# Four attention layers on one core: weight blocks asked for two ahead, layer-norm rows normed one ahead, one more unread matmul per row tile in layers 3 and 4

## The chip, the core and the metric

The kernel runs on one core of a Trainium2 chip. A core has a matrix engine (TensorE, PE in the profile; the loading of its stationary operand is listed apart as PEld), a vector engine (VectorE, DVE), a scalar engine (ScalarE, ACT), a general engine (GpSimd, POOL) and an engine that here only starts transfers (SyncE, SP). Each runs its own stream of instructions in order, and semaphores make one wait for another. The metric is the device time of one execution in microseconds (us), and lower is better. Before the change it is 2338.05 us, the median of four runs from 2328.9 to 2343.6 us.

## What is computed

A sequence of 2048 positions with 640 features goes through four layers. Each is `x = x + attention(layernorm(x))` with 32 heads of 20 features. Layers 1 and 3 use the weights A and a sliding window of 256 keys, layers 2 and 4 the weights B and all 2048 keys without a mask.

```python
def layer(x, wqkv, wo, windowed):                 # x: (1, 2048, 640)
    q, k, v = split_heads(layernorm(x) @ wqkv)    # 32 heads of 20
    s = einsum("bhqd,bhkd->bhqk", q, k) * 20 ** -0.5
    if windowed: s = where(0 <= qi - ki < 256, s, -1e9)
    return x + merge_heads(softmax(s) @ v) @ wo

x = layer(layer(A_x, A_wqkv, A_wo, True), B_wqkv, B_wo, False)
x = layer(layer(x,   A_wqkv, A_wo, True), B_wqkv, B_wo, False)
```

`layernorm` subtracts the mean of a position's 640 features and divides by `sqrt(var + 1e-5)`.

## The kernel before

**Tiling.** The code counts layers `l` from 0 to 3, so layer 3 of the text is `l = 2`. Positions are cut into four chunks `c` of 512, a chunk into four row tiles of 128 positions, and heads into eight groups `g` of four. A unit is one (layer, chunk, group). Its scores come in banks: one head's 512 queries against 128 keys fill one PSUM bank (128 partitions x 512 values). There are eight banks; score tiles use banks 0 to 2 and 3 to 5 by turns (banks 3 to 6 in a wide tile), and bank 7 collects probabilities times values. In the early part, in which every second tile has two banks, all other matmuls share banks 5 and 6; after `end_early` (line 265), which comes when the layer norms of layers 1 and 2 are done, they have bank 6 alone.

**The main loop** (from line 1210) is worked through when the kernel is built; what the chip gets is one fixed stream for each engine. One pass is called a tick here. It issues the score matmuls of the next tile of up to three banks (line 1244), one Exp on ACT for that tile (line 1275), then some other work, then the probability-times-value matmuls of an earlier tile (line 1308), then the mask products on DVE for windowed tiles (line 1344). There are 1635 ticks, and units of neighbouring layers are interleaved, so that the layer norms, projections and output projections of one layer stand between the attention ticks of another.

**The other work** consists of generators, called tasks. `pump` (line 241) lets the task that is due first advance while a credit lasts; the credit grows at each tick by a rate that is worked out from the work left and when it is due. A task gives the credit back what it costs (`yield ("pe", 0.22)`), or steps aside for n ticks (`yield ("wait", n)`). `take_m` (line 253) hands out a PSUM bank for such work; after `end_early` a bank that was given back in a tick is to be had in the next tick only, so that at most one such piece of work is done per tick.

**Tasks that the change touches:**

- `t_ln` (line 376) is one chunk's layer norm. POOL works out the reciprocal deviation (lines 387 and 390) from statistics that DVE left. Then for each of the four row tiles DVE norms the row into the tile `xn` (line 399; the pool `xnp` has two buffers), the task waits a tick, PE transposes the 128x640 row in five 128x128 pieces into a bank (line 410), and DVE, or ACT in the early part, copies the bank to `xnT` (`evac`, lines 302 and 304). In layers 1 and 2 two unread matmuls come ahead of the transposes.
- `unread` (line 609) multiplies a 128x128 identity with a 128x512 tile into a bank that nobody reads, and adds 1.0 to `heat`. `keep_clock` (line 623) does the same at the end of a tick while the `heat` that the tick's work and a carry of at most 3.0 add up to is under a minimum. These unread matmuls are there for the TensorE clock, which the page lists as the granted clock.
- `take_w` (line 329) hands a 128-column block of the q and k weights to a projection (`t_block`, line 500, and `t_qk_first`, line 485). `worder[l, n]` lists the blocks of layer l in order of use, with n = 0 for q and 1 for k. A block is fetched by `get_w` (line 312), in layer 1's first chunk by copies on DVE and a memset on POOL, otherwise by a transfer that POOL starts. `wtiles` holds the blocks that are fetched and not yet taken. When a block is taken and none of its list is in `wtiles`, the next of the list is fetched. The pool `wqkp` has eight buffers.
- A projection's result is copied to `st` and stored by a transfer that POOL starts as well (line 509), as are the value tiles (line 467). POOL's stream holds these stores, the weight fetches and the layer norms' two small operations, in one order.

In the code below `x_sb` holds the residual stream, `ps` the eight banks, and `ka` serves at times as the output of wide Exp tiles.

Of the kernel before, what the change touches and what calls it, by code (L numbers as in the profile page):

```python
# [49 lines left out]
def kernel(  # L50
# [202 lines left out]
    def take_m():  # L253
        while True:
            b = min(mfree, key=mfree.get)
            if mfree[b][0] <= state["tick"]:
                mfree[b] = (1 << 30, 0)
                return b
            yield ("wait", 1)

    def drop_m(b):
        mseq[0] += 1
        mfree[b] = (state["tick"] + (not state["early"]), mseq[0])
# [22 lines left out]
    def room(*tags):  # L286
        while any(live[t] + tags.count(t) > cap[t] for t in tags):
            yield ("wait", 1)
        for t in tags:
            live[t] += 1  # L290
        state["running"].holds = True
# [8 lines left out]
    def evac(out_, in_):  # L300
        if state["act"]:
            nc.scalar.copy(out=out_, in_=in_)
        else:
            nc.vector.tensor_copy(out=out_, in_=in_)  # L304


    wtiles = {}
# [4 lines left out]
    def get_w(l, n, c, i):  # L312

        t = wqkp.tile([P, KD, P], BF16, name="wqk", tag="wqk")
        wtick[l, n, c, i] = state["tick"] + 4
        if l or c:
            a = n * D + i * P
            nc.gpsimd.dma_start(out=t[:], in_=wq_view[l % 2][:, :, a : a + P])
            return t
        tv = t[:].rearrange("p c (j m) -> p c j m", j=4)  # L320
        nc.gpsimd.memset(tv[:, :, :, DH:32], 0.0)
        src = raw[:, :, n * D + 80 * i : n * D + 80 * (i + 1)]
        nc.vector.tensor_copy(
            out=tv[:, :, :, 0:DH], in_=src.rearrange("p c (j e) -> p c j e", j=4)
        )
        wtick[l, n, c, i] = 0
        return t

    def take_w(l, n, c, i):
        key, order = (l, n, c, i), worder[l, n]  # L330
        if key not in wtiles:
            wtiles[key] = get_w(*key)
        while state["tick"] < wtick[key]:
            yield ("wait", 1)
        at = order.index(key)
        order.pop(at)
        wt = wtiles.pop(key)
        if at < len(order) and not any(e in wtiles for e in order):
            wtiles[order[at]] = get_w(*order[at])
        return wt  # L340

    staging = []
# [33 lines left out]
    def t_ln(l, c):  # L376
        while ("x", l, c) not in ready:
            yield ("wait", 1)
        yield from room("xnT", "ln")
        for n in (1, 0):  # L380
            order = worder[l, n]
            if order and not any(e in wtiles for e in order):
                wtiles[order[0]] = get_w(*order[0])
        users[l, c] = 9 if (l, c) == (0, 0) else (11, 12, 11, 11)[l]
        mv = mvs.pop((l, c))
        rstd = lnp.tile([P, 4], F32, name="rstd", tag="rstd")
        nc.gpsimd.tensor_scalar(  # L387
            out=rstd[:], in0=mv[:, :, 1], scalar1=EPS, scalar2=1.0, op0=ALU.add, op1=ALU.mult
        )
        nc.gpsimd.tensor_tensor(out=rstd[:], in0=rstd[:], in1=nhalf[:], op=ALU.pow)  # L390
        yield ("wait", 2)
        nmr = lnp.tile([P, 4], F32, name="nmr", tag="nmr")
        nc.vector.scalar_tensor_tensor(
            out=nmr[:], in0=mv[:, :, 0], scalar=-1.0, in1=rstd[:], op0=ALU.mult, op1=ALU.mult
        )
        xt = xtp.tile([P, KD, C], BF16, name="xnT", tag="xnT")
        for i in range(4):
            xn = xnp.tile([P, D], BF16, name="xn", tag="xn")
            nc.vector.tensor_scalar(
                out=xn[:], in0=x_sb[:, 4 * c + i, :],  # L400
                scalar1=rstd[:, i : i + 1], scalar2=nmr[:, i : i + 1],
                op0=ALU.mult, op1=ALU.add,
            )
            yield ("wait", 1)
            mb = yield from take_m()
            for _ in range(2*(l<2)):
                unread(mb)
            trp = ps[:, mb, :].bitcast(BF16)[:, 0 : KD * P].rearrange("p (c m) -> p c m", c=KD)
            for dc in range(KD):
                nc.tensor.transpose(  # L410
                    out=trp[:, dc, :], in_=xn[:, dc * P : (dc + 1) * P], identity=ident[:]
                )
            evac(xt[:, :, i * P : (i + 1) * P], trp)
            drop_m(mb)
            yield ("pe", 0.4)
        xnT[l, c] = xt
        live["ln"] -= 1
        ready.add(("xnT", l, c))
# [66 lines left out]
    def t_qk_first(l, c, g):  # L485
        while ("xnT", l, c) not in ready:
            yield ("wait", 1)
        yield from room("qa", "ka", "w", "w")
        wt = yield from take_w(l, 0, c, g)
        q = qa_free.popleft()  # L490
        yield from project(wt, xnT[l, c], lambda: q[:])
        wt = yield from take_w(l, 1, c, g)
        k = ka_free.popleft()
        yield from project(wt, xnT[l, c], lambda: k[:])
        live["w"] -= 2
        qa[c, g], ka[c, g] = q, k
        used(l, c)
        ready.add(("qk", l, c, g))

    def t_block(l, n, c, b):  # L500

        while ("xnT", l, c) not in ready:
            yield ("wait", 1)
        yield from room("w")
        wt = yield from take_w(l, n, c, b)
        yield from project(wt, xnT[l, c], staged)
        rows = slice(b * P, (b + 1) * P)
        dst = k_d[l][rows, c * C : (c + 1) * C] if n else q_d[l][c, rows, :]
        nc.gpsimd.dma_start(out=dst, in_=staging.pop())
        live["w"] -= 1  # L510
        used(l, c)
        ready.add(("qk"[n], l, c, b))
# [65 lines left out]
    def push_layer(l, c):  # L578

        need = [first_use(l, c, g) for g in range(G)]  # L580
        if c or l:
            push(("ln", l, c), t_ln(l, c), need[0], 1.6)
        if l % 2:
            halves = ((0,), (1,)) if l == 1 else ((0, 1),)
            for h in halves:
                push(("v", l, c, *h), t_v(l, c, h), need[4 * h[0]], 2.8 * len(h))
        elif c or l:
            push(("v", l, c), t_v(l, c, (0, 1)), need[0], 5.6)
        if c or l:
            for b in range(KD):  # L590
                g = b * P // 80
                for n in (1, 0):
                    worder[l, n].append((l, n, c, b))
                    first = index[l, c, g, PARTS[l][0] if l % 2 and c == 0 else None]
                    first = need[g] if n else first
                    push(("qk"[n], l, c, b), t_block(l, n, c, b), first, 1.1)
            return
        for g in range(G):
            for n in (0, 1):
                worder[l, n].append((l, n, c, g))  # L600
            push(("qk", l, c, g), t_qk_first(l, c, g), need[g], 2.2)
            if g == 0:
                push(("v", l, c), t_v(l, c, (0, 1)), need[0], 5.6)
# [5 lines left out]
    def unread(b):  # L609

        nc.tensor.matmul(  # L611
            ps[:, b, :], lhsT=ident[:], rhs=masks[:, 0, :], start=True, stop=True
        )
        state["heat"] += 1.0
# [522 lines left out]
    with tc.manual_schedule():  # L1137
# [17 lines left out]
        while n < last_layer:  # L1155
            size = 2 if len(tiles) % 2 and narrow(banks[n][0]) else 3
            u = banks[n][0]
            at = placed.setdefault(id(u), [])
# [51 lines left out]
        while ended is None or t < ended + 8:  # L1210
# [3 lines left out]
            if t < len(tiles) or banks:  # L1214
# [54 lines left out]
                i = 0  # L1269
                while i < n_b:  # L1270
# [8 lines left out]
                    i = k  # L1279
# [52 lines left out]
            if t > 0 and masked is not None:  # L1332
                cur_, pt_ = masked
                i = 0
                while i < len(cur_):
# [12 lines left out]
                    i = k  # L1348
# [36 lines left out]
```

## Time and profile before

The times are those of the page: the profiled execution took 2340.73 us by the device's clock, and the span of its trace, from its first to its last instruction, is 2339.0 us; 1.7 us lie around it.

| What | Value |
|---|---|
| median of the four runs | 2338.05 us |
| profiled execution, its span | 2340.73 us, 2339.0 us |
| ACT busy | 2178.4 us, 93% of the span |
| PE busy | 2016.7 us, 86% |
| DVE busy | 1463.5 us, 63% |
| POOL busy | 271.1 us, 12% |
| Exp on ACT (line 1275) | 2099.8 us in 1641 instructions |
| unread matmuls (line 611) | 256.5 us in 768 instructions |
| row norms on DVE (line 399) | 29.8 us, 60 of 497 ns |
| transposes of the layer norm (line 410) | 30.1 us in 150 listed records, 300 with their loads |
| weight fetches started by POOL (line 318) | 150, landing 3.7 us (B) and 3.3 us (A) after issue |

The page's row of busy tenths cuts the span into 40 slices of 58.5 us. PE's durations in it are from start to modelled end, and matmuls overlap, so a PE share near 90% does not say that the array does nothing but useful work. In the row of the granted clock, 9 stands for a share of 90% or more, and the last third of the span, where layer 4 is alone, has 5. Windows of the trace give by stage:

| Stretch of the span | PE busy | DVE busy | ACT busy | granted clock |
|---|---|---|---|---|
| 0 to 130 us | 112.57 | 87.37 | 92.60 | 0.95 |
| 130 to 400 us | 251.68 | 191.29 | 238.61 | 0.99 |
| 400 to 560 us | 140.94 | 67.06 | 150.71 | 1.00 |
| 560 to 1690 us | 974.28 | 652.39 | 1074.42 | 0.96 |
| 1690 to 2339 us | 537.19 | 465.38 | 622.07 | 0.55 |

The fifteen layer norms that `t_ln` does lie between 51 and 1569 us. The seven of layers 1 and 2 are done by 442 us, the eight of layers 3 and 4 start at about 568, 794, 842, 1077, 1125, 1342, 1408 and 1563 us.

### The profile page before, as it was taken

Reading aid. Unit: us, or ns where it says so; the run is one execution under the profiler, and the core shown is the slowest. Engines: PE = TensorE matmul, PEld = TensorE weight load, DVE = VectorE, ACT = ScalarE, POOL = GpSimd, SP = SyncE. Lnnn points to the kernel's source line nnn. Section 1 sums busy time; section 2 is a strip of 40 time slices with the busy share of each in tenths; the row PEclk is TensorE's granted clock in tenths of the full one; section 3 lists DMA queues with packets and bytes.
Section 4 is the critical chain, followed back from the end, with each engine's and each line's share of the span. In section 5 each row is a group of like instructions: output and inputs, shape, how many; then the busy total and the mean of one; then the engine's idle time right before and its main releaser. Section 6 shows DMA issues by size and latency. Waiting matters only on the chain.

```text
span 2339.0 us, 40587 instructions
## 1 busy us (share of the span) xinstructions
PE 2016.7 (86%) x15773; PEld 724.9 (31%) x15773; DVE 1463.5 (63%) x2724; ACT 2178.4 (93%) x1753; POOL 271.1 (12%) x445
## 2 busy tenths in 40 slices
PE   8899999988889888888888888888888888888887
PEld 3443333333323332333323333333322222212222
DVE  6577775426646666656666544452577777777772
ACT  7788889899999988999899899999999999999997
POOL 3332321110200112001120013001000000000000
PEclk9899999999999989999999999999855565556556
DMA  6232322222300223102230033112210010011100
GB/s 183 81 95 82 104 67 63 76 71 59 89 19 27 58 63 95 43 14 58 75 99 27 13 83 109 39 31 76 63 32 27 26 38 27 27 34 39 31 14 12
DMA packets 84881, 132.57 MB, mean 57 GB/s; under 512 B 19760, under 2 KB 60080, under 8 KB 84688
## 3 DMA queue, kind: packets, MB, share of 16 engines
q1 hardware_dynamic: 65472, 76.80, 11.9%
q0 software_dynamic: 19216, 53.17, 7.8%
q8 instruction: 124, 2.03, 0.4%
q14 instruction: 69, 0.57, 0.1%
HBM read 98.70 MB, written 27.79 MB: 54 GB/s over the span
## 4 chain that ended last, share of the span: by engine, by line
ACT 41%; PE 27%; issue 16%; DVE 14%; DMA 1%; POOL 0%; ACTq 0%; SPq 0%; DVEq 0%; POOLq 0%
ACT pt L1275 40%; PE ps L1244 7%; PE ps L353 5%; PE ps L532 4%; PE ps L1308 4%; DVE pt L1344 3%; PE ps L446 3%; PE ps L611 2%; DVE on L1043 1%; DVE st L304 1%; DVE oT L830 1%; ACT ka L1275 1%; DMA wqk<-in_B_wqkv_dram 1%; DVE raw_o L878 1%; PE ps L410 1%
## 5 line engine op out<-in xcount | busy, mean ns | idle before, releaser
L1275 ACT ACTIVATE pt<-ps 128x1536 bf16<-128x1536 f32 (+2 forms) x1641 | 2099.8, 1501 | 115.4 <-PE ps L1244 103.1
L1244 PE MATMUL ps<-qt,kt 32*128 32x512 bf16 x4008 | 642.9, 456 | 196.7 <-ACT pt L1275 164.7
L1308 PE MATMUL ps<-pt,vt 128*21 128x512 bf16 x3860 | 467.2, 456 | 0.8 <-DVE raw_o L816 0.5
L1244 PEld LDWEIGHTS <-kt 32*128 32x128 bf16 x4008 | 191.4, 93 | 614.3 <-issue 591.3
L1344 DVE TENSOR_TENSOR pt<-pt,masks 128x1024 bf16<-128x1024 bf16 (+5 forms) x403 | 238.8, 626 | 127.6 <-ACT pt L1275 127.0
L611 PE MATMUL ps<-masks,ident 128*128 128x512 bf16 x768 | 256.5, 389 | 23.5 <-DVE rT L1030 9.9
L353 PE MATMUL ps<-xnT,wqk 128*128 128x512 bf16 x830 | 220.3, 390 | 20.2 <-DMA wqk<-in_B_wqkv_dram 4.9
L1308 PEld LDWEIGHTS <-vt 128*21 128x21 bf16 x3960 | 100.1, 90 | 317.1 <-issue 307.6
L304 DVE CAST st<-ps 128x512 bf16<-128x512 f32 x127 | 87.7, 691 | 156.9 <-PE ps L353 156.3
L532 PE MATMUL ps<-wop,on 128*128 128x320 bf16 x976 | 165.9, 313 | 6.8 <-DVE x_sb L541 2.5
L1244 PE MATMUL ps<-qa,ka 32*128 32x384 bf16 (+2 forms) x1408 | 116.9, 275 | 32.7 <-ACT pt L1275 27.8
L878 DVE TENSOR_SCALAR xnT<-ps 128x512 int32<-128x512 f32 x88 | 60.8, 691 | 106.4 <-PE ps L871 104.2
L1043 DVE TENSOR_TENSOR on<-oT,ps 128x512 bf16<-128x512 bf16 x128 | 87.4, 683 | 60.7 <-PE ps L1039 60.3
L830 DVE CAST oT<-ps 128x512 bf16<-128x512 f32 x112 | 76.8, 686 | 69.9 <-PE ps L1308 44.5
L446 PE MATMUL ps<-wv,xnT 128*128 128x320 bf16 x640 | 112.4, 310 | 7.6 <-DVE va L304 1.6
L541 DVE TENSOR_TENSOR x_sb<-x_sb,ps 128x320 bf16<-128x320 bf16 x120 | 57.8, 482 | 96.3 <-PE ps L532 96.2
L532 PEld LDWEIGHTS <-on 128*128 128x128 bf16 x976 | 90.3, 101 | 72.0 <-issue 38.8
L353 PEld LDWEIGHTS <-wqk 128*128 128x128 bf16 x830 | 71.6, 98 | 116.4 <-issue 51.2
L387 POOL TENSOR_SCALAR rstd<-mv 128x4 f32<-128x4 f32 x15 | 4.0, 265 | 812.5 <-DVE mv L374 812.3
L611 PEld LDWEIGHTS <-ident 128*128 128x128 bf16 x768 | 56.5, 96 | 124.0 <-issue 120.9
L1308 PE MATMUL ps<-pt,va 128*21 128x384 bf16 (+2 forms) x1408 | 78.2, 283 | 3.6 <-DVE pt L1344 2.4
L1244 PEld LDWEIGHTS <-ka 32*128 32x128 bf16 x1408 | 44.4, 92 | 101.6 <-issue 93.0
(107 smaller groups left out, 1793.5 us busy)
## 6 DMA issues: line engine op xcount, KB each, us to landing
vt<-v_d SPq DMA_DIRECT2D x48, 336.0 KB
kt<-k_d SPq DMA_DIRECT2D x192, 80.0 KB
wqk<-in_B_wqkv_dram POOLq DMA_DIRECT2D x80, 160.0 KB, 3.7
wqk<-in_A_wqkv_dram POOLq DMA_DIRECT2D x70, 160.0 KB, 3.3
k_d<-st POOLq DMA_DIRECT2D x75, 128.0 KB, 2.1
q_d<-st POOLq DMA_DIRECT2D x75, 128.0 KB, 2.1
qt<-q_d SPq DMA_DIRECT2D x384, 20.0 KB
v_d<-vs POOLq DMA_DIRECT2D x16, 336.0 KB, 3.1
```

The lines of the kernel that those rows point to most:

```text
L304: nc.vector.tensor_copy(out=out_, in_=in_)
L353: nc.tensor.matmul(pq, lhsT=wt[:, dc, :], rhs=xt[:, dc, :], start=(dc == 0), stop=(dc == KD - 1),)
L446: nc.tensor.matmul(pv, lhsT=xt[:, dc, i * P : (i + 1) * P], rhs=wv_sb[l % 2][:, dc, h * HD : (h + 1) * HD], start=(dc == 0), stop=(dc == K ...
L532: nc.tensor.matmul(yp, lhsT=on[:, g, qb * P : (qb + 1) * P], rhs=wop[:, g, i * HD : (i + 1) * HD], start=(g == g0), stop=(g == G - 1),)
L611: nc.tensor.matmul(ps[:, b, :], lhsT=ident[:], rhs=masks[:, 0, :], start=True, stop=True)
L830: nc.vector.tensor_copy(out=oT[:], in_=op)
L878: V.tensor_scalar(out=xi.bitcast(I32)[:, i * C : (i + 1) * C], in0=side["psum"], scalar1=SCALE * LOG2E * E23, scalar2=127.0 * E23, op0=ALU ...
L1043: nc.vector.tensor_tensor(out=on[:, g, :], in0=oT[:], in1=zb, op=ALU.mult)
L1244: nc.tensor.matmul(sp[:, i, col * P : (col + qn) * P], lhsT=u.k(kc, j), rhs=u.q(j, q0, qn), start=True, stop=True,)
L1275: nc.scalar.activation(out=pt[:, i:k, b0 * P :], in_=sp[:, i:k, b0 * P :], func=ACT.Exp, scale=SCALE,)
L1308: nc.tensor.matmul(op[32 * j : 32 * j + VW, q0 * P : (q0 + qn) * P], lhsT=u.v(kc, j), rhs=pg[:, i, col * P : (col + qn) * P], start=(first ...
L1344: nc.vector.tensor_tensor(out=pt_[:, i:k, b0 * P :], in0=pt_[:, i:k, b0 * P :], in1=mv_, op=ALU.mult,)
```

## The change

It has three parts. `take_w` looks at the next two blocks of the list instead of one, and fetches each that is missing while fewer than two of the list are held and fewer than four blocks in all. In `t_ln` the first row is normed ahead of the task's one-tick wait, and each later row ahead of the transposes of the row before it; the one-tick wait that each row had is left only ahead of the first. And the count of unread matmuls per row tile changes from two in layers 1 and 2 and none in layers 3 and 4 to two and one.

```diff
@@ take_w
         at = order.index(key)
         order.pop(at)
         wt = wtiles.pop(key)
-        if at < len(order) and not any(e in wtiles for e in order):
-            wtiles[order[at]] = get_w(*order[at])
+        for e in order[at : at + 2]:
+            if e not in wtiles and sum(o in wtiles for o in order) < 2 and len(wtiles) < 4:
+                wtiles[e] = get_w(*e)
         return wt
@@ t_ln
-        for i in range(4):
+
+        def normed(i):
             xn = xnp.tile([P, D], BF16, name="xn", tag="xn")
             nc.vector.tensor_scalar(
                 out=xn[:], in0=x_sb[:, 4 * c + i, :],
                 scalar1=rstd[:, i : i + 1], scalar2=nmr[:, i : i + 1],
                 op0=ALU.mult, op1=ALU.add,
             )
-            yield ("wait", 1)
+            return xn
+
+        rows = deque([normed(0)])
+        yield ("wait", 1)
+        for i in range(4):
+            if i < 3:
+                rows.append(normed(i + 1))
+            xn = rows.popleft()
             mb = yield from take_m()
-            for _ in range(2*(l<2)):
+            for _ in range(1+(l<2)):
                 unread(mb)
```

## The prediction

> **What bounds the kernel now.** I read the chain that ended last first, then the costliest groups, the waits, and windows around the layer norms.
>
> ```profile
> ACT 41%; PE 27%; issue 16%; DVE 14%; DMA 1%; POOL 0%; ACTq 0%; SPq 0%; DVEq 0%; POOLq 0%
> ```
> ```profile
> L1275 ACT ACTIVATE pt<-ps 128x1536 bf16<-128x1536 f32 (+2 forms) x1641 | 2099.8, 1501 | 115.4 <-PE ps L1244 103.1
> L1244 PE MATMUL ps<-qt,kt 32*128 32x512 bf16 x4008 | 642.9, 456 | 196.7 <-ACT pt L1275 164.7
> ```
>
> No engine holds the chain alone. ACT is 93% busy, and its Exp sat idle 115.4 us, 103.1 of them for score matmuls. So anything that makes PE's scores earlier can bring at most some 100 us, and PE work counts only where ACT waits for PE. By stage ACT is idle 37.4 us before 130 us, 31.4 to 400, 9.3 to 560, 55.6 to 1690, and 26.9 after that, where no layer norm or weight fetch is left: the change cannot touch the last 649 us.
>
> Equal windows of 16 us around the eight layer norms of layers 3 and 4 (columns: window, length, busy us and count of PE, PEld, DVE, ACT and POOL, granted clock, DMA share, GB/s):
>
> ```profile
> 567.00:583.00 16.00, 12.35 (x84) 4.69 (x83) 11.56 (x22) 12.32 (x10) 4.87 (x8) 0.68 0.36 74
> 793.00:809.00 16.00, 14.04 (x118) 5.60 (x118) 9.90 (x22) 15.88 (x14) 6.56 (x10) 1.00 0.68 149
> 841.00:857.00 16.00, 14.79 (x89) 5.61 (x89) 9.75 (x18) 11.38 (x8) 0.49 (x4) 0.57 0.08 15
> 1076.00:1092.00 16.00, 13.14 (x117) 5.31 (x117) 9.98 (x21) 15.71 (x14) 6.75 (x10) 1.00 0.66 147
> 1124.00:1140.00 16.00, 14.11 (x108) 5.75 (x105) 10.76 (x20) 13.25 (x10) 1.01 (x5) 0.79 0.10 20
> 1341.00:1357.00 16.00, 13.24 (x120) 5.54 (x120) 12.78 (x28) 15.45 (x13) 4.87 (x8) 1.00 0.48 91
> 1407.00:1423.00 16.00, 13.62 (x122) 5.81 (x120) 6.78 (x15) 16.00 (x13) 6.38 (x12) 1.00 0.46 105
> 1562.00:1578.00 16.00, 14.07 (x125) 6.39 (x122) 6.52 (x14) 16.00 (x13) 4.67 (x7) 1.00 0.45 85
> ```
>
> Where the granted clock stays 1.00, ACT loses 0.12, 0.29, 0.55, 0 and 0 us of 16. In the three where it falls, ACT loses 3.68, 4.62 and 2.75, together 11.05 us. That is where the unread matmuls can earn something. Narrow windows put the falls at 572.8 to 583.0, 842.4 to 856.1 and 1129.1 to 1136.0: nine steps of 3.4 us.
>
> **Part 1, an unread matmul per row in layers 3 and 4.** It adds 8 x 4 = 32 matmuls. As each counts 1.0 as heat, the kernel's own clock keeping drops some: the built streams have 788 in all against 768, so 12 go elsewhere. Where two stand together, the next PE work starts 0.21 us after one, so 32 are 6.9 us of PE time, or twice that at half clock. In the five warm windows PE is busy 13.1 to 14.1 of 16 us, with 1.9 to 2.9 us spare against 4 x 0.21 = 0.84, and some rows wait for `xn` anyway: free. In a window that stays cold, 4 x 0.43 = 1.7 us have 1.2 to 3.7 spare. I charge +1.5 us in all; the ends are 0 and +6.9.
>
> What it brings depends on what makes the clock fall. PE just ahead of the third fall:
>
> ```profile
> 1125.67 0.39 PE L1244 MATMUL ps<-qt,kt 32*128 32x512 bf16 x3
> 1126.57 0.44 PE L410 MATMUL ps<-ident,xn 128*128 128x128 bf16 x5 [0.51 <-DVE vs L304]
> 1126.94 0.39 PE L1244 MATMUL ps<-qt,kt 32*128 32x512 bf16 x3
> 1128.46 0.45 PE L410 MATMUL ps<-ident,xn 128*128 128x128 bf16 x5 [1.13 <-DVE xn L399]
> ```
>
> PE works, but thinly: between 1125.7 and 1129.1 it has ten transposes, six score matmuls on 32 rows and four value matmuls on 21 columns, and no full 128x128 matmul. The Trainium skill, page "TensorE: Matmul & The Clock Gate", sections "What's actually happening" and "HAM oscillation", ties the fall to an idle window of about 3.4 us and says to avoid PE gaps longer than that. This speaks against the change: the longest gaps here are 2.81, 0.85 and 1.13 us, so by that rule there would be no fall, nothing to cure, and the sum would be the +1.5 alone. The trace differs: the clock fell three times, so I follow the row: load counts, not only gaps. The page's penalty, throttled time x (1 - 1/2), makes 30.8 x 0.5 = 15.4 us of PE time of these falls; ACT's rows say 11.05, and I use these.
>
> The unread matmuls do not fill the wait for the first norm, which stays (2.81 us at 569 to 572). Later rows come about one per tick, so a window of 3.4 us gets two. I assume that five of the nine cold steps remain: 4/9 x 11.05 = 4.9, taken as **-4.5 us**; ends 0 and -10.5.
>
> **Part 2, norming one row ahead.** The waits it aims at:
>
> ```profile
> PEld L410 <- DVE xn L399: 23.4, 40, 3.1
> PE ps L410 <- DVE xn L399: 6.9, 10, 2.8
> PEld L353 <- DMA wqk<-in_B_wqkv_dram: 7.0, 7, 1.7
> PE ps L353 <- DMA wqk<-in_B_wqkv_dram: 4.9, 5, 1.4
> ```
>
> PEld's 23.4 us is no loss: in layers 1 and 2 the two unread matmuls run meanwhile. Real PE gaps ahead of the transposes sum in layers 3 and 4 to 4.2 us for first rows, which the change leaves (the first norm is issued where it was), and 4.15 us for rows 1 to 3, which go. Part lies in the cold windows already counted: **-1 us**, ends 0 and -4. Late next is the row's statistics and POOL's two operations ahead of the first norm.
>
> The new order on DVE is norm(i+1), then copy(i). Norm(i+1) takes the buffer that transposes(i-1) read, and copy(i-1) stood ahead of it with the same wait, so no new wait arises where DVE copies. Copy(i) is 0.44 us later; bank 6 is asked for again a tick of about 1.6 us later, which covers it. In the first 78 ticks ACT copies instead, and DVE waits for PE itself, with mask products (line 1344) behind it: three layer norms, nine norms.
>
> The dropped one-tick waits also pack rows. With banks 5 and 6 both free in layers 1 and 2, the built order has nine ticks with two rows and one with three, where before each had one. In layers 3 and 4 bank 6 alone keeps it to one per tick. One row is two unread matmuls and five transposes, 2 x 0.21 + 0.45 = 0.87 us. The work is the same and ticks beside become lighter, so **0**, ends -5 and +10. In layers 1 and 2 two copies of the early part move from ACT to DVE (585 and 431 ns); half of that counts: **-0.5 us**.
>
> **Part 3, two weight blocks ahead.** PE waited 11.9 us for B's blocks, in twelve waits. Why they are late:
>
> ```profile
> 449.54 0.76 POOL L467 DMA_DIRECT2D v_d<-vs  x1 [4.35 <-issue]
> 450.95 0.86 POOL L318 DMA_DIRECT2D wqk<-in_B_wqkv_dram  x1 [0.65 <-PE ps L1244]
> 451.80 0.57 POOL L509 DMA_DIRECT2D k_d<-st  x1
> ```
>
> The fetch stands behind a store whose data came late; it lands 3.7 to 4.7 us after issue, and PE waited 1.45 us for it at 455.2. Five such fetches are pieces of 3.4 to 4.4 us in the chain. One block earlier the fetch stands ahead of that store. The 150 fetches stay (0.87 us of POOL each), and two or four now come in a row, up to 3.5 us ahead of a store; POOL is 12% busy and nobody waits for these stores at once. Eight buffers hold four taken and four fetched blocks. A fetch now waits somewhat more often for the buffer's last matmul: by the streams, 11 fetches have under three Exp instructions between, before 5. Fetches with at most four Exp instructions to first use fall from 29 to 16. I take 8 of 11.9 us of PE time, half of it on ACT's clock: **-4 us**; ends 0 and -11.
>
> **The sum:** +1.5 - 4.5 - 1 + 0 - 0.5 - 4 = -8.5 us. From the profiled 2340.73 that is 2332.2; that run lies 2.7 us over the median of 2338.05, so in medians 2329.6: **2330 us**.
>
> **The rivals.** A kernel's difference of under 0.5% (11.7 us) is about what a measurement cannot tell from no change.
>
> - *More than that, faster* (0.36 for under 2326.4): the three falls go wholly and the weight waits too, -10.5 - 11 - 4 + 1.5 = -24, or 2314. For it: five layer norms already cost nothing when warm. Against: first rows still wait, and waits on PE do not all reach ACT.
> - *Hidden anyway* (with my forecast 0.41 within 0.5%): the falls move instead of going, because 12 unread matmuls are missing elsewhere; each further fall of 3.4 us costs ACT about 1.3 us (1190 to 1204 shows two). The weights and row waits alone leave 2334.
> - *Slower* (0.23 over 2349.7): the packed rows decide. The score matmuls of the next tile stand behind two or three rows in PE's order. Eleven rows move into a tick that has one already, 11 x 0.87 = 9.6 us; in ten ticks norm and copy (0.44 + 0.49) hold DVE while mask products wait, 9.3 more, and with half of the +6.9 exposed 3.4: 2330 + 22.3 = 2352. It decides once PE's lead of one score tile there is under 0.9 us. For it: ACT is idle 69 us before 400 us. Against: the lighter ticks beside it.
> - *Not what it says:* in layers 1 and 2 the count of unread matmuls stays two, so that part is nothing there; this is in the sum.
>
> The likeliest's own range is 2324 to 2337. The range for 8 in 10 goes to 2314 and 2352, the rivals' times.
>
> **What would show it.** Right: windows at the layer norms of layers 3 and 4 with a clock over 0.8 and ACT idle under 2 us each; waits of line 353 for `wqk` under 5 us; ACT idle before 400 us unchanged within 5 us. Wrong: as many 3.4 us falls as before at other places, ACT idle before 400 us up by 10, or a first norm that still costs 3 to 5 us in each cold layer norm.

## The result, and the profile after

The changed kernel takes 2330.15 us (median of 36 runs, 2324.28 to 2340.02) against 2338.08 us for the kernel before (57 runs, 2328.9 to 2351.14). The ratio is 0.9966, with a 95% interval from 0.9956 to 0.9975: 8 us less, between 5.8 and 10.3. The forecast was 2330 us. The experiments show, however, that the time came from another part of the change than the sum said.

The profiled execution took 2325.45 us, 4.7 us under the median, while the profiled run of before lay 2.7 us over its own. The two pages therefore show about 15 us of difference where medians show 8. The chain that ended last and the groups of Exp and of the score matmuls, of the changed kernel (its lines are numbered nine higher from line 418 on):

```profile
ACT 41%; PE 27%; issue 14%; DVE 12%; DMA 0%; POOL 0%; ACTq 0%; SPq 0%; DVEq 0%; POOLq 0%
```
```profile
L1284 ACT ACTIVATE pt<-ps 128x1536 bf16<-128x1536 f32 (+2 forms) x1641 | 2098.5, 1503 | 107.1 <-PE ps L1253 101.1
L1253 PE MATMUL ps<-qt,kt 32*128 32x512 bf16 x4008 | 639.4, 453 | 193.4 <-ACT pt L1284 161.9
```

The chain has the same make-up, with less "issue" and less DVE, and weight transfers are gone from it. Exp is as long as before and waits 8 us less.

The eight layer norms of layers 3 and 4 in the changed kernel, in windows of 16 us that begin, to the nearest us, at the same Exp instruction as those shown before (columns as there: busy us and count of PE, PEld, DVE, ACT and POOL, granted clock, DMA share, GB/s):

```profile
564.00:580.00 16.00, 12.80 (x85) 4.99 (x85) 12.00 (x24) 12.11 (x10) 6.90 (x10) 0.68 0.44 98
789.00:805.00 16.00, 13.75 (x117) 5.57 (x116) 9.33 (x21) 15.72 (x13) 3.30 (x6) 1.00 0.48 108
837.00:853.00 16.00, 13.70 (x112) 6.03 (x112) 9.99 (x19) 13.81 (x11) 2.67 (x6) 0.89 0.30 52
1072.00:1088.00 16.00, 13.88 (x121) 5.82 (x121) 11.01 (x23) 16.00 (x14) 5.66 (x9) 1.00 0.64 137
1119.00:1135.00 16.00, 14.29 (x127) 6.46 (x126) 10.43 (x20) 14.98 (x12) 0.10 (x1) 1.00 0.13 23
1328.00:1344.00 16.00, 13.97 (x123) 5.93 (x122) 13.11 (x28) 15.54 (x13) 5.02 (x8) 1.00 0.49 92
1393.00:1409.00 16.00, 15.13 (x129) 6.43 (x128) 7.94 (x17) 15.96 (x13) 8.40 (x14) 1.00 0.55 129
1546.00:1562.00 16.00, 14.74 (x125) 6.78 (x122) 6.67 (x14) 16.00 (x13) 4.90 (x8) 1.00 0.47 89
```

Two of the three cold windows are warm or nearly so: the third and the fifth line have 0.89 and 1.00 of the clock, where before they had 0.57 and 0.79. The first, at layer 3's first layer norm, is as it was. From 560 us to the Exp instruction that stands at 1690 us before, the granted clock is 0.98 in place of 0.96. ACT idle in the eight windows sums to 7.9 us of 128, before 12.0.

And PE's waits for a normed row and for weight blocks of B:

```profile
PEld L419 <- DVE xn L401: 11.3, 14, 2.8
PE ps L419 <- DVE xn L401: 3.5, 7, 1.4
PEld L354 <- DMA wqk<-in_B_wqkv_dram: 1.4, 1, 1.4
PE ps L354 <- DMA wqk<-in_B_wqkv_dram: 1.1, 1, 1.1
```

Both are much shorter, 14.8 us in place of 30.3 and 2.5 in place of 11.9. From these lines alone one would say that all three parts worked, and would credit each with a share. That is what the experiments were for.

### The profile page after: what moved, and what is told of

It is laid out like the page before. It is cut to its first block, busy times and chain, and to the rows that moved or that the text cites. A ratio compares the mean times of both kernels' runs of the same rounds, so it can differ in the third digit from the quotient of the medians.

```text
span 2323.7 us, 40627 instructions
## 1 busy us (share of the span) xinstructions
PE 2006.6 (86%) x15793; PEld 723.6 (31%) x15793; DVE 1465.7 (63%) x2726; ACT 2175.7 (94%) x1751; POOL 273.8 (12%) x445
## 4 chain that ended last, share of the span: by engine, by line
ACT 41%; PE 27%; issue 14%; DVE 12%; DMA 0%; POOL 0%; ACTq 0%; SPq 0%; DVEq 0%; POOLq 0%
ACT pt L1284 40%; PE ps L1253 7%; PE ps L354 5%; PE ps L541 4%; PE ps L1317 4%; DVE pt L1353 3%; PE ps L455 3%; PE ps L620 2%; DVE on L1052 1%; DVE st L304 1%; ACT ka L1284 1%; DVE raw_o L887 1%; DVE oT L839 1%; PE ps L419 1%; DVE x_sb L550 1%
## 5 line engine op out<-in xcount | busy, mean ns | idle before, releaser
L620 PE MATMUL ps<-masks,ident 128*128 128x512 bf16 x788 | 266.8, 391 | 29.3 <-DVE rT L1039 11.5
L1253 PE MATMUL ps<-qa,ka 32*128 32x384 bf16 (+2 forms) x1408 | 117.3, 276 | 30.3 <-ACT pt L1284 25.5
L455 PE MATMUL ps<-wv,xnT 128*128 128x320 bf16 x640 | 107.5, 300 | 10.3 <-DVE rz L1025 3.8
```

The lines of the kernel that those rows point to most:

```text
L455: nc.tensor.matmul(pv, lhsT=xt[:, dc, i * P : (i + 1) * P], rhs=wv_sb[l % 2][:, dc, h * HD : (h + 1) * HD], start=(dc == 0), stop=(dc == K ...
L620: nc.tensor.matmul(ps[:, b, :], lhsT=ident[:], rhs=masks[:, 0, :], start=True, stop=True)
L1253: nc.tensor.matmul(sp[:, i, col * P : (col + qn) * P], lhsT=u.k(kc, j), rhs=u.q(j, q0, qn), start=True, stop=True,)
```

## The experiments

Each kernel was timed beside runs of the kernel before on the same chip. The three parts are called N (norms one row ahead, with the dropped waits), U (the unread matmul in layers 3 and 4) and W (weights two ahead). A kernel's ratio to the runs of before beside it is known to about 0.0015 either way, which is 3.5 us.

### Part by part, and leaving one out

**U alone.** The kernel before with one edit:

```diff
-            for _ in range(2*(l<2)):
+            for _ in range(1+(l<2)):
```

> The kernel before with the unread matmul per row tile in layers 3 and 4 alone. Theory A (the sum as predicted): the clock is granted longer in these layer norms, -3 us against before (0.9987), with the three cold windows of 16 us at 0.8 or more granted clock. Rival B (all of the gain comes from earlier weights): no change or +1.5 us for the added PE work (1.000 to 1.0006). Rival C (the gain comes from the order that happens to be built, not from any part): a difference of either sign up to 5 us, with no link to the clock in the layer norms.

Measured: 0.9996 (0.998 to 1.0013), no difference. The unread matmul alone brings nothing that shows. Yet it did what it is for: in the kernel's one profile, of a run 8.7 us under its median, the three cold layer norms are warmer and ACT gets more done in them.

```profile
562.00:578.00 16.00, 12.59 (x89) 4.98 (x88) 11.73 (x23) 12.42 (x10) 4.87 (x8) 0.79 0.36 77
...
839.00:855.00 16.00, 14.28 (x121) 6.24 (x120) 10.38 (x21) 14.89 (x11) 2.43 (x6) 1.00 0.18 37
...
1122.00:1138.00 16.00, 14.79 (x118) 6.35 (x116) 10.91 (x20) 14.28 (x11) 1.62 (x5) 0.92 0.14 25
```

Over the eight windows ACT is busy 4.7 us more than before. More work done in these windows is thus not yet a shorter run.

**N and W, without U.** The changed kernel with `range(2*(l<2))`.

> The changed kernel without the unread matmul in layers 3 and 4 (weights two ahead and norms one ahead stay). Theory A: -5.5 us against before (0.9976), and falls of the clock in the layer norms of layers 3 and 4 come back. Rival B: the full -8 us (0.9966). Rival C: anything between -8 and +5.

Measured: 0.9967 (0.9955 to 0.9978), the whole gain. Theory A had 0.9976 for it.

**N alone.** The kernel before with the new `normed` and `rows` in `t_ln`, and with `range(2*(l<2))` and the old `take_w`.

> The kernel before with the norms one row ahead alone, two and no unread matmuls as before. Theory A: -1.5 us (0.9994). Rival B: 0. Rival D (packed rows in layers 1 and 2 cost what the other parts bring): +4 to +10 us (1.0017 to 1.004), with more ACT idle time before 400 us.

Measured: 0.9961 (0.9945 to 0.9977). Theories A, B and D all fall: the part that the sum gave 1.5 us brings everything. ACT idle time before 400 us did not rise. In the profile the gain lies between the Exp instructions that stand at 560 and 1690 us before: 1123 us in place of 1131. But PE's waits for a normed row, 30.3 us before, hardly fell:

```profile
PEld L418 <- DVE xn L400: 17.5, 23, 3.1
PE ps L418 <- DVE xn L400: 9.3, 9, 2.8
```

In layers 3 and 4 the PE gaps ahead of rows 1 to 3 went from 4.15 to 1.8 us, and those ahead of first rows from 4.2 to 4.9. Of the 8 us measured, this profile shows 1.6 as PE gaps that are gone.

**N and U, without W.** The changed kernel with the old `take_w`:

```diff
-        for e in order[at : at + 2]:
-            if e not in wtiles and sum(o in wtiles for o in order) < 2 and len(wtiles) < 4:
-                wtiles[e] = get_w(*e)
+        if at < len(order) and not any(e in wtiles for e in order):
+            wtiles[order[at]] = get_w(*order[at])
```

> The changed kernel with one weight block ahead as before. Theory A: -4.5 us against before (0.998), and PE waits of some 12 us for weight blocks of B come back. Rival B: 0 (1.000). Rival D: +4 or more.

Measured: 0.9964 (0.9949 to 0.9978). And PE's waits for blocks of B did not come back: they are 4.7 us, before 11.9. N by itself had moved the order enough to shorten them to 5.5:

```profile
PEld L353 <- DMA wqk<-in_B_wqkv_dram: 3.6, 7, 1.6
...
PE ps L353 <- DMA wqk<-in_B_wqkv_dram: 1.9, 2, 1.3
```

These lines are the waits of the kernel with N alone.

**U and W, without N.** The kernel before with the new `take_w` and `range(1+(l<2))`.

> The kernel before with weights two ahead and the unread matmul in layers 3 and 4, the norms as before. Theory N (formed after the first four runs: the norms one row ahead bring all of it): no difference, 1.000 within 0.0015. Theory A (parts add up): what the changed kernel has less the norms, -7 us (0.997).

Measured: 0.9998 (0.9982 to 1.0014). Without N the two other parts together bring nothing.

Seven of the eight combinations are thus known; W alone was not tried. Each part can be read as a difference of pairs:

| Part | Without, with | Without, with | Without, with | Mean effect |
|---|---|---|---|---|
| N | 1.0000, 0.9961 | U: 0.9996, 0.9964 | U and W: 0.9998, 0.9966 | -0.0034, 8 us |
| U | 1.0000, 0.9996 | N: 0.9961, 0.9964 | N and W: 0.9967, 0.9966 | -0.0001 |
| W | U: 0.9996, 0.9998 | N: 0.9961, 0.9967 | N and U: 0.9964, 0.9966 | +0.0003 |

N is the change. The three values of each row agree within 0.0007, closer than the intervals of single ratios. This does not exclude rival C, that the order which happens to be built decides: N changes that order.

### Which half of N, and where

N does two things in each layer norm: a row is normed before PE comes to it, and the waits of a tick are dropped, so that rows come earlier. Four kernels take these apart.

**The norms ahead, the waits kept.** On the kernel with N alone:

```diff
         for i in range(4):
+            if i:
+                yield ("wait", 1)
             if i < 3:
                 rows.append(normed(i + 1))
```

Its rows stand in the same ticks as in the kernel before.

> The kernel before with each row normed ahead of the transposes of the row before, but with the one-tick wait of every row kept, so that the order of everything else stays as it was and no rows are packed. If the gain comes from rows that are ready when PE asks: -8 us (0.9965). If it comes from the dropped waits (packed rows in layers 1 and 2, layer norms done ticks earlier): 0 to -2 us (0.999 to 1.000).

Measured: 0.9979 (0.9965 to 0.9993), 5 us.

**The waits dropped, the norms not ahead, in layers 3 and 4.** From the second row on each row is normed right ahead of its own transposes there; layers 1 and 2 are as before.

```diff
         for i in range(4):
-            if i < 3:
-                rows.append(normed(i + 1))
+            if i:
+                rows.append(normed(i))
+                if l < 2:
+                    yield ("wait", 1)
             xn = rows.popleft()
```

> The kernel before with the one-tick waits dropped in layers 3 and 4, but each row still normed right ahead of its own transposes. Its rows stand in the same ticks as in the kernel with norms ahead in layers 3 and 4 alone (0.9971). If a row that is ready when PE asks is what brings the gain: slower than before, 24 rows each waiting some 0.5 us for their norm, 1.002 to 1.005. If the dropped waits bring it: 0.997 to 0.998.

Measured: 0.9988 (0.9972 to 1.0004). A theory of ready rows alone had it slower, at 1.002 to 1.005, one of dropped waits alone at 0.997 to 0.998. It is neither.

**N in layers 3 and 4 alone, and N in layers 1 and 2 alone.** The loop of N where `l >= 2`, or where `l < 2`, and the old one elsewhere.

> Norms one row ahead, with the waits dropped, in layers 3 and 4 alone. If rows that are ready, and fewer thin windows of PE, keep the clock there: -5 to -8 us (0.9965 to 0.998), with ACT idle time from 560 to 1690 us down. If the gain lies in layers 1 and 2: 0 to -2 us.

Measured: 0.9971 (0.9957 to 0.9986), most of the gain.

> Norms one row ahead, with the waits dropped, in layers 1 and 2 alone. If packing in the early part is what helps: -6 to -8 us (0.9965 to 0.9975), with ACT idle time between 130 and 400 us down by some 4 us. If the gain lies in layers 3 and 4: 0 or slower by up to 5.

Measured: 0.9995 (0.998 to 1.0009): the packed rows of the early part neither help nor hurt, which was the forecast's value for them.

So N works in layers 3 and 4. The kernel with the waits dropped there and the one with N there alone have their rows in the same ticks and differ by the norms alone: 0.9988 without them ahead, 0.9971 with. In their traces PE waits, with the norm just in time,

```profile
PEld L425 <- DVE xn L400: 24.0, 39, 3.1
...
PE ps L425 <- DVE xn L400: 8.8, 14, 2.8
```

and with the norm one row ahead,

```profile
PEld L425 <- DVE xn L400: 16.7, 28, 3.1
PEld L425 <- DVE xnT L304: 2.0, 6, 0.4
PE ps L425 <- DVE xn L400: 6.8, 6, 2.8
```

The PE rows (the matmul itself late) fall from 14 waits, 13 of them in layers 3 and 4, to 6; of these only the three first rows, 4.9 us, lie in layers 3 and 4, and the longest is 2.8 us in both kernels. The norms ahead give some -0.002 in both settings (0.9979 against 1.0000, 0.9971 against 0.9988), the dropped waits some -0.001 (0.9988 against 1.0000, 0.9971 against 0.9979). Only the first of these four differences is clear of the noise; the others are known to some 0.002 either way.

The granted clock shows another side. Runs of the kernel with the waits kept have on average 677 us at half clock, those of before beside them 690; with the waits dropped and the norms not ahead it is 701 against 692. By the slope of the last section, 0.31 us of time for each us at half clock, an estimate is that the clock brings 4 us of the first kernel's gain of 5, and takes 3 us from the second, which would be some 5 us faster than before otherwise. At equal clock the dropped waits would be the larger half. How the two halves share the gain is not settled.

The windows of the three cold layer norms, in the kernel with N in layers 3 and 4 alone:

```profile
566.00:582.00 16.00, 12.66 (x93) 5.13 (x94) 12.13 (x23) 12.90 (x11) 4.87 (x8) 0.68 0.32 73
...
840.00:856.00 16.00, 14.91 (x111) 6.19 (x105) 9.38 (x17) 14.26 (x10) 0.00 (x0) 0.72 0.17 26
...
1124.00:1140.00 16.00, 14.91 (x114) 6.24 (x111) 10.05 (x19) 13.91 (x11) 0.00 (x0) 0.79 0.15 26
```

ACT is busy 12.90, 14.26 and 13.91 us, where before it was 12.32, 11.38 and 13.25, together 4.1 us more. PE did 93, 111 and 114 matmuls in place of 84, 89 and 108. The clock is still low in all three: 0.68 and 0.79 as before in the first and third, and 0.72 in place of 0.57 in the second, where the fall is shorter and most of the 4.1 us lie. In the second and third PE is busy 14.9 of 16 us while ACT waits 1.7 and 2.1, which suggests that PE is the bound there and that a gap ahead of a row is lost whole. How much of the second window's gain is the gap and how much the shorter fall, one profile does not tell.

### Later first rows

The first row of each layer norm still made PE wait, so two kernels gave it one more tick:

```diff
         rows = deque([normed(0)])
-        yield ("wait", 1)
+        yield ("wait", 1 + (l >= 2))
```

On the changed kernel:

> The changed kernel with a wait of two ticks instead of one after the first norm in layers 3 and 4, so that PE should not stand before the first row either. If first rows still cost what the trace shows (2 to 4 us of PE gaps, and the fall of the clock at about 568 us): 2 to 4 us faster than the changed kernel, 0.995 of before. If the later end of the layer norms costs as much: 0.9966 or slower.

Measured: 0.9991 (0.9972 to 1.001). On N in layers 3 and 4 alone:

> Norms one row ahead in layers 3 and 4 alone, with the same longer first wait, no unread matmuls there and weights as before. If the clock's fall at the first layer norm of layer 3 comes from PE's gap before the first row: ACT idle time there from 3 to under 1.5 us, and 2 to 4 us faster than without the longer wait, 0.9955 of before. Otherwise 0.997.

Measured: 0.9998 (0.9982 to 1.0013). Both lose most or all of the gain. The wait itself did what it should in the first of them, as its windows of the three layer norms show:

```profile
565.00:581.00 16.00, 12.38 (x106) 5.41 (x106) 12.50 (x24) 14.10 (x12) 8.66 (x12) 0.89 0.52 115
...
836.00:852.00 16.00, 14.05 (x102) 5.98 (x102) 10.32 (x19) 12.77 (x10) 0.49 (x4) 0.79 0.09 17
...
1120.00:1136.00 16.00, 14.55 (x115) 6.45 (x113) 11.29 (x21) 14.10 (x11) 2.05 (x6) 0.89 0.15 29
```

At the first layer norm ACT is busy 14.10 us in place of 12.11 and the clock is 0.89 in place of 0.68. PE gaps ahead of first rows, 2.0 us in layers 3 and 4 of the changed kernel, are zero. But the layer norms of layers 3 and 4 end one or two ticks later in the built order, and what the first window gains the second and third lose (12.77 and 14.10 against 13.81 and 14.98). Outside the windows no single place holds the rest.

The second kernel is the sharper case. Its windows of the three layer norms:

```profile
562.00:578.00 16.00, 12.77 (x90) 4.99 (x91) 12.35 (x25) 13.33 (x11) 6.69 (x10) 0.69 0.46 99
...
842.00:858.00 16.00, 13.41 (x123) 6.37 (x120) 11.16 (x22) 14.93 (x11) 0.65 (x5) 1.00 0.09 18
...
1124.00:1140.00 16.00, 13.42 (x121) 6.31 (x120) 11.34 (x21) 15.33 (x12) 1.26 (x5) 1.00 0.13 25
```

At the first the PE gap is 1.3 us in place of 2.8, yet the clock falls as before. The other two are fully warm without U. ACT is busy 2.5 us more in the three than with N in layers 3 and 4 alone, and over all eight windows 6.2 us more than before. Still this kernel is some 6 us slower than that one. The loss lies elsewhere: from 560 to 1690 us its clock is 0.96, as before, so falls at other places took the place of those that are gone. The windows show what N does at the layer norms; they do not add up to the time.

So later rows hurt. That a layer norm's end sets the work behind it fits this, but no trace of the work behind it shows it, and it cannot be all: in the built order the changed kernel's layer norms end one tick earlier in three of eight cases and no earlier in the others, and with the waits kept none ends earlier, though that kernel gained 5 us. Rival C stays open in this form: N brings its gain in five orders that have it in layers 3 and 4, and one more tick takes most of it away in two.

### What the unread matmul does

The combinations say that U brings nothing. To see why, one kernel keeps the changed kernel's instruction stream, but its 32 unread matmuls in layers 3 and 4 use a quarter of the array's rows:

```diff
-            ps[:, b, :], lhsT=ident[:], rhs=masks[:, 0, :], start=True, stop=True
+            ps[:, b, :], lhsT=ident[0:rows, :], rhs=masks[0:rows, 0, :], start=True, stop=True
```

with `rows` at 32 where `t_ln` calls it for layers 3 and 4, and 128 elsewhere.

> The changed kernel with the same instruction stream, but the 32 unread matmuls of layers 3 and 4 use 32 rows of the array instead of 128: the same count and length, less load. If they earn by the clock what they cost in PE time (a fit of time against the granted clock over all runs says some 5 us each way): 4 to 6 us slower than the changed kernel, 0.9985 of before, with more time at half clock in those layer norms. If neither load nor place matters: as the changed kernel, 0.9966.

Measured: 1.0002 (0.9986 to 1.0017). Against the changed kernel (0.9966) it is 8 us slower by nothing but the rows that an unread matmul fills; against the changed kernel without U (0.9967) it is 8 us slower by unread matmuls that bring a quarter of the load. Each of these differences is known to some 4.5 us either way. Its windows of the three layer norms, and then those of the kernel without U:

```profile
562.00:578.00 16.00, 12.85 (x82) 4.21 (x82) 11.66 (x21) 11.40 (x9) 6.89 (x10) 0.66 0.43 94
...
837.00:853.00 16.00, 14.45 (x99) 5.45 (x95) 9.29 (x16) 12.53 (x9) 2.02 (x6) 0.69 0.29 47
...
1123.00:1139.00 16.00, 15.63 (x106) 5.62 (x102) 9.38 (x18) 12.33 (x10) 0.00 (x0) 0.68 0.14 25
```
```profile
565.00:581.00 16.00, 12.04 (x82) 4.57 (x82) 12.25 (x24) 12.21 (x10) 6.89 (x10) 0.70 0.44 99
...
842.00:858.00 16.00, 14.92 (x110) 6.28 (x106) 9.38 (x17) 13.98 (x10) 0.00 (x0) 0.71 0.04 9
...
1126.00:1142.00 16.00, 15.50 (x110) 6.29 (x107) 9.62 (x17) 13.99 (x10) 0.00 (x0) 0.73 0.08 13
```

The clock is nearly the same, 0.66 to 0.73 in all six. With the twelve unread matmuls of low load ACT is busy 0.81, 1.45 and 1.66 us less, together 3.9: a good 0.3 us each, three quarters of the 0.43 us that the prediction has for one at half clock. Over all eight windows ACT's busy time is 4.6 us less than without U; the rest of the 8 us is not located. With full load, in the changed kernel, the clock of the second and third window is 0.89 and 1.00 and the cost is made up. Whole runs agree: the narrow kernel has on average 706 us at half clock and the changed one 681, and 25 us at 0.31 are some 8 us, an estimate. That is what U does: it buys the clock back at about the price that the bought clock is worth.

### Why earlier weights bring nothing

W did shorten PE's waits, in the kernel with U and W from 11.9 to 7.6 us. Between the two Exp instructions that stand at 450 and 470 us before, that kernel is 2.9 us faster. But it has a late fetch of its own elsewhere. PE's and POOL's rows of its timeline:

```profile
282.65 1.25 PE L354 MATMUL ps<-xnT,wqk 128*128 128x512 bf16 x5 [1.40 <-DMA wqk<-in_B_wqkv_dram]
```
```profile
277.31 0.76 POOL L468 DMA_DIRECT2D v_d<-vs  x1 [0.76 <-issue]
278.06 0.86 POOL L318 DMA_DIRECT2D wqk<-in_B_wqkv_dram  x1
```

The fetch stands behind a store again, and PE stands 1.40 us. Between the Exp instructions at 280 and 290 us of before that kernel is 2.6 us slower, and between those at 40 and 60 us, in layer 1's first chunk, 1 to 2 us. These losses do not cancel all that W gains in layers 1 and 2: at 560 us the kernel is 4.1 us ahead of before in its profile, and it loses 3.4 of it after that. One profile cannot weigh this: the kernel with U alone has the PE stream of before up to 571 us, and in its profile it is 4.8 us ahead at 560, with 6.8 us at half clock up to there in place of 20.5. That no gain of W is left over is measured; why is not shown.

## Why the prediction was right

The time was right, the direction was right, and the place was wrong. Of the sum of -8.5 us the terms came out so:

- **The bound** fits: in the changed kernel Exp is as long as before and waits less for PE, and the norms bring their gain in layers 3 and 4. That the gain is made at the layer norms with a low clock is not shown: with U alone, and with N and a later first row in layers 3 and 4, ACT gained there as much as with N or more, and the time did not fall.
- **Part 1, -4.5 and +1.5 us.** The mechanism is confirmed: a narrow unread matmul of the same length gives 1.0002, the full one 0.9966, so load counts, as whole runs' time at half clock also says. The row was rightly preferred to the idle-window rule that the Trainium skill has on its page "TensorE: Matmul & The Clock Gate", section "What's actually happening": the clock fell with no PE gap over 2.81 us. Both sizes were too small. The load is worth about 8 us and the PE time costs about 8, each to some 4.5 us. The step that failed is "in a window that stays cold, 4 x 0.43 = 1.7 us have 1.2 to 3.7 spare": in cold windows three quarters of the added PE time was exposed, 3.9 us in three windows. In the five warm ones it was nearly free, as the sum said (0.7 us of ACT in all). U's net effect is -0.0001, not -3 us. Nor do 12 unread matmuls go elsewhere because of U: the changed kernel without U has 756, so U adds its full 32 there.
- **Part 2, -1 and -0.5 us.** This is the term that was most mis-sized: N measured -0.0034, 8 us, and -0.0029 in layers 3 and 4 alone. The sum took the PE gaps of rows 1 to 3, 4.15 us, and discounted them as already counted in the cold windows. That discount was not the error, or only a small part of it: of the 4.15 us N alone took away 2.35, and first rows lost 0.75 of that again. What failed is the reading that N is worth the PE gaps ahead of its rows. The order of work that the dropped waits build, and through it the clock, had no value in the sum. The experiments show that N brings 8 us and that most of it needs layers 3 and 4; beyond 1.6 us of PE gaps the cause stays open.
- **Packing, 0.** Right within the noise: 0.9995 in layers 1 and 2. The slower rival, packed rows, did not happen; ACT idle before 400 us is 68.7 us in the changed kernel, before 68.8.
- **Part 3, -4 us.** Wrong: W measured +0.0003. The waits fell as expected (11.9 to 2.5 us), but N alone had already brought them to 5.5, and the order that W builds has late places of its own. The step that failed is "half of it on ACT's clock": what PE no longer waits did not reach the time.
- **Not what it says** does not hold: all three parts do what they say on the engines they touch.

The total thus agrees by luck: one term was too small by about what two others were too large. The signs announced beforehand were half met: waits for weights under 5 us and an unchanged early part came true; a clock over 0.8 did in seven of eight windows, but ACT idle under 2 us in six of eight only: layer 3's first layer norm kept 3.9 us and its second 2.2. The sign against it, a first norm that still costs 3 to 5 us, came true at one of the three.

No kernel here beats the changed one clearly. N alone (0.9961, 0.9945 to 0.9977) is as fast with one part of three.

## What to carry to other kernels

When a change has several parts, a sum over them that comes out right says little about each: leave each one out. Where the clock has fallen, filler that cost nearly nothing elsewhere was paid for by three quarters here, so filler that is to keep the clock up must be priced at the low clock. Windows around the place that a change aims at can look better while the run does not: two kernels here gained 4.7 and 6.2 us of ACT's work at the layer norms and nothing in time. Norming a row one step ahead, with its waits dropped, was worth more here than either curing the clock or fetching weights sooner.

## What had not been expected of the hardware

The spread between runs of one and the same kernel follows the granted clock. In the traces the clock is either full or half. Taking the time at half clock as 2 x (1 - mean granted clock) x time, the 75 runs of the kernel before that stood beside the kernel with the waits kept lie between 2331.18 and 2353.79 us and have on average 690 us at half clock; their times rise by 0.31 us for each us of it, with a correlation of 0.98. Most of the 690 us is layer 4 alone: in the stretch from 1690 us on the profile of before has 0.55 of the clock, and ACT is busy 622 of 649 us. A single profile is therefore no measure of an effect of 0.3%: the profiled run of the kernel with U alone took 2331.9 us, though its median is 2340.66.

The clock can also be mended without a gain. Runs of the changed kernel have on average 20 us less at half clock than those of the kernel without U (681 against 701 us), and are not faster.
